# Half of the first K through ScalarE's DMA queue in float32 with a cast on chip, and batch 0's and 1's attention at other steps

## The chip, the cores and the metric

The kernel runs on one core of a Trainium2 chip. Times are device microseconds of that core. Each version is timed in rounds beside the kernel before on the same chip. A profile is of one execution; its span is about 1.8 us shorter than the time of the same run (511.5 against 513.26 us for the kernel before), so spans are compared with spans only.

## The reference

Inputs: q, k, v of 8 batches x 8 heads x 1024 tokens x 64; E and F of 64 x 1024; two FFN weights. All are float32.

```python
k_proj = einsum('ks,bhsd->bhkd', E, k)       # 1024 tokens -> 64
v_proj = einsum('ks,bhsd->bhkd', F, v)
attn   = softmax(q @ k_proj^T / 8)           # per head, over the 64
x      = attn @ v_proj                       # regrouped as (8192 tokens, 512)
out    = relu(x @ w_in) ** 2 @ w_out         # 512 -> 2048 -> 512
```

## The kernel before

All matrix work is bfloat16. GpSimd's queue loads q, k, v and the weights and casts them from float32 on the way; only E comes in float32 through SyncE's queue. The FFN of a batch runs in two halves of 512 tokens ("chunks" c), each with 16 first blocks (`fb`) of four matmuls and then the second matmuls. The order on TensorE is written by hand: the FFN is a generator that yields after each "step", and `at(step, ...)` puts pieces of the next batch's attention between steps. `warm(n)` issues n matmuls of zeros, only to keep TensorE busy.

```python
e_f32 = soft_pool.tile([KP, S], F32, tag="rs", name="e_f32")
nc.sync.dma_start(e_f32[:], E[:])
...
for g in range(2):
    load(K0[:, half[g]], tokens(k, 0, h=half[g]))            # load = nc.gpsimd.dma_start, casts
    load(Q0[:, half[g], 0:4, :], tokens(q, 0, h=half[g], i=slice(0, 4)))
    if g == 0:
        make_identity(nc, ident[:])
        load(f_bf[:], F[:])
for g in range(2):
    load(V0[:, half[g]], tokens(v, 0, h=half[g]))
# then w_in in five pieces, w_out in four, Q's second part before the last of them, batches 1, 2 ...
...
def sums(self, pr):                    # two head pairs at once
    ...                                # ones-matmuls of 32 rows into one tile
    nc.scalar.activation(rs[1][:], ps[:], AF.Ln)
    nc.scalar.activation(rs[0][:], rs[1][:], AF.Exp, scale=-1.0)
    nc.scalar.activation(rs[1][:], rs[1][:], AF.Exp, scale=-1.0)
    for j in range(2):
        for a in range(2):             # spread 32 rows to 64
            nc.vector.tensor_copy(rs[j][lack:lack + 32], rs[j][have:have + 32])
...
def chunk_sums(self, c, g):            # one at a time: Ln, Exp, no copies
    ps = att_psum()
    self.sums_mm(ps, self.e[g])
    self.rs[g] = self.inverse(ps)
```

The softmax here doesn't subtract the row's maximum and nothing guards it: scores larger than these inputs give would overflow.

Of the kernel before, what the change touches and what calls it, by code (L numbers as in the profile page):

```python
# [8 lines left out]
P = 128  # L9
F32 = mybir.dt.float32  # L10
# [8 lines left out]
def kernel(  # L19
# [49 lines left out]
    def bank(shape=(P, 512), dtype=F32):  # L69
        return fps.tile(list(shape), dtype, tag="bank", name="ps_bank")  # L70

    def tokens(src, b, h=slice(None), i=slice(None)):
        return src[b].rearrange("h (p i) d -> p h i d", i=NI)[:, h, i, :]

    def load(t, src):
        return nc.gpsimd.dma_start(t, src)  # L76
# [9 lines left out]
    e_f32 = soft_pool.tile([KP, S], F32, tag="rs", name="e_f32")  # L86
    nc.sync.dma_start(e_f32[:], E[:])

    K0, Q0, V0 = (qkv_pool.tile([P, H, NI, D], BF16, name=n) for n in ("K_sb", "Q_sb", "V_sb"))
    f_bf = soft_pool.tile([KP, S], BF16, tag="expT", name="f_bf")  # L90
    half = (slice(0, 4), slice(4, 8))
    ident = const_pool.tile([P, P], BF16, name="ident")
    for g in range(2):
        load(K0[:, half[g]], tokens(k, 0, h=half[g]))
        load(Q0[:, half[g], 0:4, :], tokens(q, 0, h=half[g], i=slice(0, 4)))
        if g == 0:
            make_identity(nc, ident[:])
            load(f_bf[:], F[:])
# [33 lines left out]
    def projection(name, e_bf):  # L132
        ps = bank([P, NI, KP], BF16)
        view = e_bf[:].rearrange("k (p i) -> k i p", i=NI)
        for i in range(NI):
            nc.tensor.transpose(ps[:, i, :], view[:, i, :], ident[0:KP, 0:KP])
        t = const_pool.tile([P, NI, KP], BF16, name=name)
        nc.vector.tensor_copy(t[:], ps[:])
        return t

    def warm(n):

        ps = bank()
        for _ in range(n):
            nc.tensor.matmul(ps[:], lhsT=zeros[:, 0:P], rhs=zeros[:], start=True, stop=True)
# [199 lines left out]
    class Ffn:  # L345
# [29 lines left out]
        def steps(self):  # L375
            for c in range(2):
                self.hsq[c] = hsq_pool.tile([P, NFB, TCH], BF16, name="hsq")
                first = self.cold and c == 0
                fb0 = 0
                if first:  # L380

                    banks = [bank() for _ in range(4)]
                    for g, fbs in ((0, (0, 1)), (0, (2, 3)), (1, (0, 1)), (1, (2, 3))):
                        for fb in fbs:
                            for cb in (2 * g, 2 * g + 1):
                                self.first_mm(c, fb, cb, banks[fb])
                            if g == 1:
                                self.square(c, fb, banks[fb])
                        yield
                    fb0 = 4  # L390
                for fb in range(fb0, NFB):
                    ps = bank()
                    for cb in range(NCB):
                        self.first_mm(c, fb, cb, ps)
                    self.square(c, fb, ps)
                    yield
                if first:

                    for t0 in range(0, 4, 2):
                        banks = [bank() for _ in range(2)]  # L400
                        for j in range(WP):
                            for t in range(2):
                                for fb in range(j * fn, (j + 1) * fn):
                                    self.second_mm(c, t0 + t, fb, banks[t])
                                if j == WP - 1:
                                    self.store(c, t0 + t, banks[t])
                                yield
                else:
                    last = self.b == B - 1 and c == 1
                    for tb in range(4):  # L410
                        if last and tb == 3:

                            for m in (slice(0, DM // 2), slice(DM // 2, DM)):
                                ps = bank()
                                for fb in range(NFB):
                                    self.second_mm(c, tb, fb, ps, m)
                                self.store(c, tb, ps, m)
                            break
                        ps = bank()
                        for j in range(WP):  # L420
                            for fb in range(j * fn, (j + 1) * fn):
                                self.second_mm(c, tb, fb, ps)
                            if j == WP - 1:
                                self.store(c, tb, ps)
                            yield

    with tc.manual_schedule(engines={PE}):
        e_bf = soft_pool.tile([KP, S], BF16, tag="expT", name="e_bf")
        nc.vector.tensor_copy(e_bf[:], e_f32[:])
        warm(8)  # L430
        ET = projection("ET", e_bf)
        warm(3)
        att = Attention(0)
        att.project_k(0)
        att.transpose_q_chunk(0, Q0, 0)
        att.transpose_k((0,))
        warm(1)
        att.chunk_scores(0, 0)
        FT = projection("FT", f_bf)
        att.project_k(1)  # L440
        att.chunk_sums(0, 0)
        att.transpose_q_chunk(0, Q0, 1)
        att.transpose_k((1,))
        warm(2)
        att.chunk_scores(0, 1)
        warm(4)
        att.project_v(0)
        att.chunk_sums(0, 1)
        warm(1)
        att.chunk_values(0, 0)  # L450
        warm(1)
        att.project_v(1)

        coming = None
        for b in range(B):
            plan = {}

            def at(step, fn, *args, **kwargs):
                plan.setdefault(step, []).append(lambda: fn(*args, **kwargs))

            if b == 0:
                at(1, att.chunk_values, 0, 1)
                at(20, att.transpose_q_chunk, 1, Q0, 0)
                at(20, att.transpose_q_chunk, 1, Q0, 1)
                at(22, att.chunk_scores, 1, 0)
                at(22, att.chunk_scores, 1, 1)
                at(25, att.chunk_sums, 1, 0)
                at(25, att.chunk_sums, 1, 1)
                at(29, att.chunk_values, 1, 0)
                at(29, att.chunk_values, 1, 1)  # L470
                nxt = Attention(1)
                nxt.load()
            if b + 1 < B:
                if b + 2 < B:
                    coming = Attention(b + 2)
                    coming.load()
                if b == 0:
                    at(36, nxt.project)
                    at(37, nxt.transpose_q, 0)
                    at(37, nxt.transpose_q, 1)  # L480
                    at(39, nxt.transpose_k)
                    at(41, nxt.scores, 0)
                    at(41, nxt.scores, 1)
                    at(43, nxt.transpose_q, 2)
                    at(43, nxt.transpose_q, 3)
                    at(45, nxt.sums, 0)
                    at(45, nxt.values, 0)
                    at(51, nxt.values, 1, True)
                    at(51, nxt.scores, 2)
                    at(51, nxt.scores, 3)  # L490
                    at(55, nxt.sums, 2)
                    at(55, nxt.values, 2)
                    at(55, nxt.values, 3, True)
                else:
                    at(14, nxt.scores, 0)
                    at(14, nxt.scores, 1)
                    at(18, nxt.sums, 0)
                    at(18, nxt.values, 0, True)
                    at(18, nxt.scores, 2)
                    at(27, nxt.values, 1)  # L500
                    at(27, nxt.scores, 3)
                    at(49, nxt.sums, 2)
                    at(49, nxt.values, 2)
                    at(49, nxt.values, 3, True)
                if b + 2 < B:
                    if b == 0:
                        at(61, coming.project)
                        at(63, coming.transpose_q_dma)
                        at(64, coming.transpose_k)
                    else:  # L510
                        at(27, coming.project)
                        at(30, coming.transpose_q_dma)
                        at(29, coming.transpose_k_dma)
            for step, _ in enumerate(Ffn(att, b == 0).steps(), 1):
                for stage in plan.pop(step, []):
                    stage()
            assert not plan, plan
            att, nxt = nxt, coming
# [30 lines left out]
```

## Time and profile before

| | kernel before |
|---|---|
| median of the first 3 runs | 513.74 us (513.23 to 514.64) |
| span of the profiled run | 511.5 us |
| first FFN matmul | 20.88 us |
| third w_in piece first used | 25.23 us |
| batch 1's first FFN matmul | 91.94 us |

From the page of the kernel before: TensorE's busy time, its granted clock and the DMA engines' share in 40 slices, and the chain of waits by engine.

```profile
PE 502.2 (98%) x2756; PEld 223.6 (44%) x2756; DVE 213.6 (42%) x433; ACT 273.7 (54%) x412; POOL 32.1 (6%) x44
...
PEclk9999999999999999999999999999999999999999
DMA  9999999899996199104931060100102011010102
...
PE 87%; DMA 11%; issue 1%; DVE 0%; POOL 0%; ACT 0%; POOLq 0%; ACTq 0%
```

TensorE is busy 98% of the span. The DMA line shows the engines full in most of the first 16 slices, which is 205 us, and rarely after. To see where TensorE lacks work, read its timeline. The columns are start, duration, engine, line, operation, output and inputs, count, and in brackets the idle time before it with what ended that. `ET` is E transposed, `xT` the attention's result, transposed, which the FFN reads; `ps_bank` and `ps_att` are TensorE's output buffers. TensorE at the start, kernel before:

```profile
5.23 0.68 PE L136 MATMUL ps_bank<-ident,e_bf 64*128 64x64 bf16 x8 [0.44 <-DVE e_bf L429]
...
7.29 1.03 PE L194 MATMUL ps_bank<-K_sb,ET 128*64 128x256 bf16 x8 [0.62 <-DMA K_sb<-in_k_dram]
...
11.85 1.88 PE L194 MATMUL ps_bank<-K_sb,ET 128*64 128x256 bf16 x8 [0.59 <-DMA K_sb<-in_k_dram]
...
20.88 1.04 PE L358 MATMUL ps_bank<-xT,w_in_114 128*128 128x512 bf16 x4
...
23.72 0.81 PE L358 MATMUL ps_bank<-xT,w_in_114 128*128 128x512 bf16 x3 [0.22 <-DVE xT L341]
...
25.23 3.62 PE L358 MATMUL ps_bank<-xT,w_in_118 128*128 128x512 bf16 x16
```

The eight K projections take 1.03 us at 7.29 us but 1.88 us at 11.85 us: the clock is halved there, which the records of the granted clock give as 0.5 from 11.92 to 15.33 us. The first FFN block over w_in_114 begins at 20.88 us, its second half waits for xT until 23.72 us, and the third piece, w_in_118, begins at 25.23 us.

TensorE's longest waits in the same trace (total, times, longest):

```profile
PE ps_bank L194 <- DMA K_sb<-in_k_dram: 1.2, 2, 0.6
...
PE ps_bank L241 <- DMA Q_sb<-in_q_dram: 0.8, 1, 0.8
PE ps_att L256 <- DVE xT L316: 0.8, 1, 0.8
PE ps_bank L231 <- DMA Q_sb<-in_q_dram: 0.7, 2, 0.4
```

Apart from the starting phase there are three: 0.82 us for batch 1's Q (L241), 0.44 us of the 0.7 for batch 0's second Q part (L231), and 0.76 us for an attention buffer that the xT multiply frees (L256). The chain of waits, in order of time (start, length, what):

```profile
3.86 7.94 DMA K_sb<-in_k_dram
...
12.09 16.78 DMA w_in_122<-in_moe_w_in_dram
...
29.15 30.96 DMA Q_sb<-in_q_dram
60.16 1.07 PE ps_bank L241 x16
```

Until 60.16 us the chain is one load after another on GpSimd's queue. From there on it is TensorE, but for the work of ScalarE and VectorE from 72.5 to 77.2 us that ends in the wait for the attention buffer.

### The profile page before, as it was taken

How to read it: one execution, taken by the hardware profiler on the slowest of the kernel's cores; microseconds unless marked ns; L12 is line 12 of the kernel's file. 1: busy time of each engine (PE TensorE's matmuls, PEld its weight loads, DVE VectorE, ACT ScalarE, POOL GpSimd, SP SyncE). 2: the span in 40 equal slices, each digit the busy share in tenths (PEclk: the TensorE clock that was granted, in tenths of full speed). 3: DMA queues.
4: the chain of work that ended last, by engine and by line, in shares of the span. 5: the costliest groups of instructions: out<-in, count | busy, mean ns of one | idle time of the engine just before them, and what ended most of it. 6: DMA issues, size and time to landing. Idle time of an engine off the chain costs nothing.

```text
span 511.5 us, 6926 instructions
## 1 busy us (share of the span) xinstructions
PE 502.2 (98%) x2756; PEld 223.6 (44%) x2756; DVE 213.6 (42%) x433; ACT 273.7 (54%) x412; POOL 32.1 (6%) x44
## 2 busy tenths in 40 slices
PE   7999999999999999999999999999999999999997
PEld 3444444444444444444444444444444444444444
DVE  2441666544444445345352354434443443522130
ACT  2565475673637556375654837366472755544351
POOL 7320100121000020001000000000000000000000
PEclk9999999999999999999999999999999999999999
DMA  9999999899996199104931060100102011010102
GB/s 161 204 205 222 227 207 201 129 217 205 195 214 124 43 183 210 71 0 91 201 88 45 1 161 16 60 24 32 63 1 81 2 41 42 25 59 21 62 1 82
DMA packets 67840, 53.92 MB, mean 105 GB/s; under 512 B 29152, under 2 KB 59616, under 8 KB 67808
## 3 DMA queue, kind: packets, MB, share of 16 engines
q0 software_dynamic: 30880, 29.49, 36.4%
q1 hardware_dynamic: 36928, 23.99, 17.8%
q8 instruction: 21, 0.34, 0.3%
q14 instruction: 11, 0.09, 0.1%
HBM read 59.24 MB, written 16.78 MB: 149 GB/s over the span
## 4 chain that ended last, share of the span: by engine, by line
PE 87%; DMA 11%; issue 1%; DVE 0%; POOL 0%; ACT 0%; POOLq 0%; ACTq 0%
PE ps_bank L364 40%; PE ps_bank L358 40%; DMA Q_sb<-in_q_dram 6%; DMA w_in_122<-in_moe_w_in_dram 3%; PE ps_bank L185 2%; DMA K_sb<-in_k_dram 2%; PE ps_att L256 1%; PE ps_att L290 1%; PE ps_att L312 1%; PE ps_bank L312 1%; PE ps_bank L241 0%; DVE rs L300 0%; ACT rs L296 0%; POOL K_sb L76 0%; DVE xT L316 0%
## 5 line engine op out<-in xcount | busy, mean ns | idle before, releaser
L355 DVE TENSOR_TENSOR hsq<-h_relu 128x512 bf16<-128x512 bf16 x256 | 108.7, 425 | 192.5 <-ACT h_relu L354 191.8
L354 ACT ACTIVATE h_relu<-ps_bank 128x512 bf16<-128x512 f32 x256 | 151.8, 599 | 69.5 <-PE ps_bank L358 69.4
L364 PEld LDWEIGHTS <-hsq 128*128 128x128 bf16 x1040 | 99.7, 98 | 122.9 <-issue 9.3
L371 ACT COPY o_sb<-ps_bank 128x512 f32<-128x512 f32 (+1 forms) x65 | 37.5, 579 | 111.1 <-PE ps_bank L364 105.0
L364 PE MATMUL ps_bank<-w_out_128,hsq 128*128 128x512 bf16 (+1 forms) x260 | 65.8, 376 | 0.0
L364 PE MATMUL ps_bank<-w_out_124,hsq 128*128 128x512 bf16 (+1 forms) x260 | 65.7, 376 | 0.0
L364 PE MATMUL ps_bank<-w_out_131,hsq 128*128 128x512 bf16 (+1 forms) x260 | 65.6, 376 | 0.0
L364 PE MATMUL ps_bank<-w_out_126,hsq 128*128 128x512 bf16 (+1 forms) x260 | 65.6, 376 | 0.0
L358 PE MATMUL ps_bank<-xT,w_in_122 128*128 128x512 bf16 x256 | 59.1, 379 | 0.0
L358 PE MATMUL ps_bank<-xT,w_in_118 128*128 128x512 bf16 x256 | 58.2, 379 | 0.0
L358 PE MATMUL ps_bank<-xT,w_in_120 128*128 128x512 bf16 x256 | 58.2, 379 | 0.0
L300 DVE COPY rs<-rs 32x1024 f32<-32x1024 f32 x56 | 38.6, 690 | 42.3 <-ACT rs L295 41.5
L270 ACT ACTIVATE expT<-ps_att 128x1024 bf16<-128x1024 f32 x32 | 31.8, 1023 | 25.3 <-PE ps_att L256 25.2
L358 PEld LDWEIGHTS <-w_in_122 128*128 128x128 bf16 x256 | 24.5, 98 | 31.2 <-issue 2.7
L358 PEld LDWEIGHTS <-w_in_120 128*128 128x128 bf16 x256 | 24.9, 98 | 30.1 <-issue 0.4
L358 PEld LDWEIGHTS <-w_in_118 128*128 128x128 bf16 x256 | 24.9, 98 | 29.9 <-issue 0.4
L358 PE MATMUL ps_bank<-xT,w_in_114 128*128 128x512 bf16 x128 | 30.6, 379 | 0.2 <-DVE xT L341 0.2
L358 PE MATMUL ps_bank<-xT,w_in_116 128*128 128x512 bf16 x128 | 30.4, 379 | 0.0
L316 DVE TENSOR_TENSOR xT<-ps_att,rs 128x512 bf16<-128x512 f32 x28 | 18.1, 686 | 9.2 <-PE ps_att L312 8.9
L294 ACT ACTIVATE rs<-ps_att 128x1024 f32<-128x1024 f32 x14 | 14.3, 1023 | 12.7 <-PE ps_att L290 12.7
L358 PEld LDWEIGHTS <-w_in_114 128*128 128x128 bf16 x128 | 12.4, 98 | 15.3 <-issue 0.9
L358 PEld LDWEIGHTS <-w_in_116 128*128 128x128 bf16 x128 | 12.4, 98 | 15.1 <-issue 0.2
(71 smaller groups left out, 236.6 us busy)
## 6 DMA issues: line engine op xcount, KB each, us to landing
out_dram<-o_sb SPq DMA_DIRECT2D x63, 256.0 KB, 2.0
K_sb<-in_k_dram POOLq DMA_DIRECT2D x7, 1024.0 KB, 22.2
V_sb<-in_v_dram POOLq DMA_DIRECT2D x7, 1024.0 KB, 26.7
Q_sb<-in_q_dram POOLq DMA_DIRECT2D x7, 1024.0 KB, 14.8
K_sb<-in_k_dram POOLq DMA_DIRECT2D x2, 512.0 KB, 7.0
V_sb<-in_v_dram POOLq DMA_DIRECT2D x2, 512.0 KB, 11.1
Q_sb<-in_q_dram POOLq DMA_DIRECT2D x2, 256.0 KB, 7.5
w_in_118<-in_moe_w_in_dram POOLq DMA_DIRECT2D x1, 512.0 KB, 14.9
```

The lines of the kernel that those rows point to most:

```text
L185: nc.tensor.matmul(ps[LO, :], lhsT=ET[:, i, :], rhs=self.K[:, :, i, :], start=f, stop=l)
L256: nc.tensor.matmul(ps[o, par], lhsT=self.kT[r, h % 4, h // 4, :], rhs=self.qT[r, h, n, :], start=True, stop=True)
L270: nc.scalar.activation(e[:], ps[:], AF.Exp, scale=SCALE)
L294: nc.scalar.activation(rs[1][:], ps[:], AF.Ln)
L300: nc.vector.tensor_copy(rs[j][lack:lack + 32], rs[j][have:have + 32])
L312: nc.tensor.matmul(ps_x[par][o], lhsT=self.vp[r, 2 * pr + a, :], rhs=e[r, par], start=True, stop=True)
L316: nc.vector.tensor_tensor(out=self.xT[:, pr, :, par], in0=ps_x[par].rearrange("p (c t) -> p c t", c=2), in1=rs[:, par].rearrange("p (c t) ...
L354: nc.scalar.activation(r[:], ps[:], AF.Relu)
L355: nc.vector.tensor_tensor(out=self.hsq[c][:, fb, :], in0=r[:], in1=r[:], op=ALU.mult)
L358: nc.tensor.matmul(ps[:], lhsT=w_in_blk(cb, fb), rhs=self.xT[:, cb, c].rearrange("p a t -> p (a t)"), start=(cb == 0), stop=(cb == NCB - 1),)
L364: nc.tensor.matmul(ps[:, m], lhsT=self.hsq[c][:, fb, tb * P:(tb + 1) * P], rhs=w_out_blk(fb)[:, m], start=(fb == 0), stop=(fb == NFB - 1),)
L371: nc.scalar.copy(o[:, m], ps[:, m])
```

## The change

The intent is to bring batch 0's first K half in over a second queue, so that the other loads begin one transfer earlier, and to place the attention of batches 0 and 1 so that TensorE never waits for a load.

```diff
+    k_f32 = []
+    for j in range(2):
+        t = soft_pool.tile([P, 2, NI, D], F32, tag="rs", name="k_f32")
+        nc.scalar.dma_start(t[:], tokens(k, 0, h=slice(2 * j, 2 * j + 2)))
+        k_f32.append(t)
...
     for g in range(2):
-        load(K0[:, half[g]], tokens(k, 0, h=half[g]))
+        if g == 1:
+            load(K0[:, half[g]], tokens(k, 0, h=half[g]))
...
-                    banks = [bank() for _ in range(4)]
-                    for g, fbs in ((0, (0, 1)), (0, (2, 3)), (1, (0, 1)), (1, (2, 3))):
-                        for fb in fbs:
+                    banks = [bank() for _ in range(2)]
+                    for g in range(2):
+                        for fb in range(2):
...
-                    fb0 = 4
+                    fb0 = 2
...
         nc.vector.tensor_copy(e_bf[:], e_f32[:])
+        nc.vector.tensor_copy(K0[:, 0:2], k_f32[0][:])
+        nc.scalar.copy(K0[:, 2:4], k_f32[1][:])
...      # warm(n) in the start: 3 -> 4 after ET, 0 -> 1, 1 -> 3, 0 -> 3 after FT, 4 -> 2, 0 -> 1, 1 -> 0
             if b == 0:
-                at(20, att.transpose_q_chunk, 1, Q0, 0)      # and ..., 1)
-                at(22, att.chunk_scores, 1, 0)               # and 1, 1
-                at(25, att.chunk_sums, 1, 0)                 # and 1, 1
+                at(21, att.transpose_q_chunk, 1, Q0, 0)
+                at(23, att.chunk_scores, 1, 0)
+                at(26, att.sums, 0)
...
-                    at(37, nxt.transpose_q, 0)               # and 1
+                    at(39, nxt.transpose_q, 0)
-                    at(43, nxt.transpose_q, 2)               # and 3
+                    at(44, nxt.transpose_q, 2)
-                    at(45, nxt.values, 0)
-                    at(51, nxt.values, 1, True)
-                    at(51, nxt.scores, 2)
+                    at(48, nxt.values, 0, True)
+                    at(48, nxt.scores, 2)
+                    at(51, nxt.values, 1)
```

More of the change, by code (lines that the diff above doesn't have):

```diff
@@ L429 @@
         nc.vector.tensor_copy(e_bf[:], e_f32[:])
+        nc.vector.tensor_copy(K0[:, 0:2], k_f32[0][:])
+        nc.scalar.copy(K0[:, 2:4], k_f32[1][:])
         warm(8)
         ET = projection("ET", e_bf)
-        warm(3)
+        warm(4)
         att = Attention(0)
         att.project_k(0)
+        warm(1)
         att.transpose_q_chunk(0, Q0, 0)
         att.transpose_k((0,))
-        warm(1)
+        warm(3)
         att.chunk_scores(0, 0)
         FT = projection("FT", f_bf)
+        warm(3)
         att.project_k(1)
@@ L445 @@
         att.chunk_scores(0, 1)
-        warm(4)
+        warm(2)
         att.project_v(0)
+        warm(1)
         att.chunk_sums(0, 1)
-        warm(1)
         att.chunk_values(0, 0)
@@ L462 @@
                 at(1, att.chunk_values, 0, 1)
-                at(20, att.transpose_q_chunk, 1, Q0, 0)
-                at(20, att.transpose_q_chunk, 1, Q0, 1)
-                at(22, att.chunk_scores, 1, 0)
-                at(22, att.chunk_scores, 1, 1)
-                at(25, att.chunk_sums, 1, 0)
-                at(25, att.chunk_sums, 1, 1)
+                at(21, att.transpose_q_chunk, 1, Q0, 0)
+                at(21, att.transpose_q_chunk, 1, Q0, 1)
+                at(23, att.chunk_scores, 1, 0)
+                at(23, att.chunk_scores, 1, 1)
+                at(26, att.sums, 0)
                 at(29, att.chunk_values, 1, 0)
@@ L478 @@
                     at(36, nxt.project)
-                    at(37, nxt.transpose_q, 0)
-                    at(37, nxt.transpose_q, 1)
+                    at(39, nxt.transpose_q, 0)
+                    at(39, nxt.transpose_q, 1)
                     at(39, nxt.transpose_k)
@@ L483 @@
                     at(41, nxt.scores, 1)
-                    at(43, nxt.transpose_q, 2)
-                    at(43, nxt.transpose_q, 3)
+                    at(44, nxt.transpose_q, 2)
+                    at(44, nxt.transpose_q, 3)
                     at(45, nxt.sums, 0)
-                    at(45, nxt.values, 0)
-                    at(51, nxt.values, 1, True)
-                    at(51, nxt.scores, 2)
+                    at(48, nxt.values, 0, True)
+                    at(48, nxt.scores, 2)
+                    at(51, nxt.values, 1)
                     at(51, nxt.scores, 3)
```

## The prediction

> **What bounds the kernel now.** TensorE: busy 98% of a 511.5 us span (the page's first part), and the chain of waits is TensorE matmuls back to back from 60.2 us to the end. In the timeline, 16 steady 512-column matmuls take 3.45 us at a granted clock of 1.00, gapless after 77.6 us. The diff leaves batches 2 to 7 alone, so only the first 78 us can change. There the chain is one DMA queue: loads land back to back until 60.2 us at about 205 GB/s of bfloat16 (windows view), twice that as float32 read.
>
> **What can be won,** by TensorE's timeline:
> - Start-up: the first FFN matmul starts at 20.88 us. K's second half is waited for until 11.85 us; from 12 to 15.5 us the granted clock is about 0.5: eight 256-column matmuls take 1.88 us, against 1.03 us for the first half. Being cold costs about 1.3 us there (0.85 + 0.4 on transposes + 0.2 on sums).
> - Three stalls: 0.44 us for Q's second part (39.6), 0.82 us for batch 1's Q (60.2), 0.76 us for a buffer that the xT multiply frees (77.2).
>
> **What the change does.**
> 1. 1 MB of float32 K leaves GpSimd's queue (one 0.89 us issue less before everything else there). The bytes read are the same. ScalarE issues it after its 1.28 us table load, so no earlier than before. The Trainium skill ("DMA: Bandwidth & Descriptors", Queues, rings and completion order) says that each engine takes its queues in turn, so K now shares with Q, F and the second K half. No run shows it yet. Casts add about 0.7 us on VectorE (64x1024 took 0.69) and an estimated 1.0 us on ScalarE (128x1024 activations take 1.02). Net: first K ready at 7.5 to 9 us (7.29 now), Q and F earlier, the second K half at 11 to 12 us.
> 2. Five more warm-up matmuls keep the clock full. "TensorE: Matmul & The Clock Gate" (Part 1) has the array drop to half clock after an idle window of about 3.4 us; the trace agrees (0.50 after a sparse stretch). Gain about 1.3 us.
> 3. Only two FFN blocks, not four, are now begun before the first group's xT is whole. That gives back about 0.8 us. Net start-up gain 0.6 us.
> 4. Q's transposes move one step (0.86 us) and batch 1's two to three steps (1.7 us) later: 0.44 + 0.82 us of stalls go.
> 5. The joint sums of batch 0 save 0.2 us of matmul, but add four 0.69 us VectorE copies before xT. Sums end near 46.2; Ln and two exponentials to 49.4, copies to 51.2, four multiplies to 53.8, while the second FFN half wants xT from 51.9: a new stall of about 1.2 us.
> 6. The new place of batch 1's values removes the 0.76 us stall.
>
> Sum: 0.6 + 1.26 + 0.2 - 1.2 + 0.76 = about 1.6 us, all on the critical path, of 513.74.
>
> **Predicted: 512.1 us, 8 in 10 between 510.4 and 514.1.** Faster by over 2%: 0.005; within 2%: 0.985; slower: 0.01.
>
> **What would show it.** Granted clock near 1.0 from 12 to 15.5 us; first FFN matmul near 19.5 us; no TensorE wait for Q; at about 52 us a TensorE wait on the xT multiply of around 1 us; no stall near 77; equal matmul spacing after 80 us.
>
> **What would make it wrong.** K on ScalarE's queue landing after 9 us (the two queues halving each other); V or w_in landing so late that a faster start only waits; the step-5 stall being absent (then about 511) or costing the clock (then above 513).

## The result, and the profile after

| | before | after |
|---|---|---|
| median | 513.52 us (6 runs, 513.23 to 514.64) | 513.00 us (6 runs, 512.56 to 513.18) |
| span of the profiled run | 511.5 us | 511.2 us |

The ratio is 0.9986, with a 95% interval of 0.9973 to 0.9999: the same within 2%, a little faster. Ratios are the mean time of one kernel's runs over the mean of the other's in the same rounds, so they are not quite the ratio of the medians.

The same lines of the page, kernel after:

```profile
PE 502.9 (98%) x2761; PEld 223.9 (44%) x2761; DVE 217.5 (43%) x438; ACT 273.7 (54%) x412; POOL 31.2 (6%) x43
...
PEclk8999999999999999999999999999999999999999
DMA  9999999899996199104941060100102011010102
...
PE 96%; DVE 1%; DMA 1%; ACT 0%; issue 0%; ACTq 0%; DVEq 0%
```

The chain of waits is now 96% TensorE, and the DMA part fell from 11% to 1%. So the change did take the loads off the chain. It still saved only half a microsecond. To see why, here is the start on TensorE, kernel after (L201 is the K projection, L365 the first FFN matmul):

```profile
6.72 0.68 PE L143 MATMUL ps_bank<-ident,e_bf 64*128 64x64 bf16 x8 [1.93 <-DVE e_bf L436]
...
8.30 1.89 PE L201 MATMUL ps_bank<-K_sb,ET 128*64 128x256 bf16 x8
...
21.36 1.04 PE L365 MATMUL ps_bank<-xT,w_in_117 128*128 128x512 bf16 x4
...
23.61 0.38 PE L365 MATMUL ps_bank<-xT,w_in_117 128*128 128x512 bf16 x1 [0.87 <-DVE xT L348]
...
26.58 3.62 PE L365 MATMUL ps_bank<-xT,w_in_121 128*128 128x512 bf16 x16
```

TensorE's longest waits after the change:

```profile
PE ps_bank L143 <- DVE e_bf L436: 1.9, 1, 1.9
PE ps_bank L365 <- DVE xT L348: 1.8, 5, 0.9
```

The waits for Q and the one for the attention buffer are gone. New ones stand in their place, for E's cast and for xT. Of the 1.8 us for xT, 0.87 and 0.22 us lie at 23.6 and 24.2 us, where two blocks are too few to fill the time until xT's second half (the kernel before, with four, waits 0.22 us there); the other three, of 0.22 us each, lie at the FFN's second half. The start across engines, kernel after (SPq and ACTq are the queues' issue instructions):

```profile
0.74 1.28 ACT L108 ACT_TABLE_LOAD   x1 [0.74 <-PEq L543]
0.74 0.57 SPq L87 DMA_DIRECT2D e_f_91<-in_E_dram  x1
0.77 0.45 ACTq L92 DMA_DIRECT2D k_f_93<-in_k_dram  x1
...
1.25 0.49 ACTq L92 DMA_DIRECT2D k_f_95<-in_k_dram  x1
...
5.96 0.71 DVE L436 CAST e_bf<-e_f_91 64x1024 bf16<-64x1024 f32 x1 [4.74 <-DMA e_f_91<-in_E_dram]
...
6.92 1.05 ACT L438 CAST K_sb<-k_f_95 128x1024 bf16<-128x1024 f32 x1 [4.89 <-DMA k_f_95<-in_k_dram]
```

E and the first K piece are issued within 0.03 us of each other, and K's issue runs while ScalarE loads its table. E's cast begins at 5.96 us (4.48 us before). The chain of waits from 0 to 90 us begins with it:

```profile
0.74 5.19 DMA e_f_91<-in_E_dram
5.96 0.72 DVE e_bf L436
```

The new wait at the FFN's second half comes from the joint sums (the softmax denominators of two head pairs at once). VectorE and then TensorE, kernel after:

```profile
49.85 2.79 DVE L307 COPY rs<-rs 32x1024 f32<-32x1024 f32 x4 [6.66 <-ACT rs L302]
52.68 2.49 DVE L348 TENSOR_TENSOR xT<-ps_att,rs 128x512 bf16<-128x512 f32 x4
```

```profile
53.43 0.38 PE L365 MATMUL ps_bank<-xT,w_in_117 128*128 128x512 bf16 x1
54.02 0.38 PE L365 MATMUL ps_bank<-xT,w_in_117 128*128 128x512 bf16 x1 [0.22 <-DVE xT L348]
54.62 0.38 PE L365 MATMUL ps_bank<-xT,w_in_117 128*128 128x512 bf16 x1 [0.22 <-DVE xT L348]
55.22 1.24 PE L365 MATMUL ps_bank<-xT,w_in_117 128*128 128x512 bf16 x5 [0.22 <-DVE xT L348]
```

VectorE spends 2.79 us on four copies of the joint sums. Then each of the first four FFN matmuls waits for its own xT multiply.

A ledger of where TensorE begins the same work in both traces (us):

| TensorE begins | before | after | after minus before | what lies between |
|---|---|---|---|---|
| first FFN matmul | 20.88 | 21.36 | +0.48 | E late, half clock earlier |
| third w_in piece | 25.23 | 26.58 | +1.35 | two blocks instead of four |
| second w_out matmuls, second pair of token blocks | 44.67 | 45.41 | +0.74 | no wait for Q |
| second half's first FFN matmul | 52.90 | 53.43 | +0.53 | joint sums |
| second half's second w_in piece | 54.63 | 56.30 | +1.67 | the wait for xT |
| second half's fourth w_in piece | 63.87 | 64.55 | +0.68 | no wait for batch 1's Q |
| after batch 1's last values | 81.99 | 81.81 | -0.18 | no wait for the buffer |
| batch 1's first FFN matmul | 91.94 | 91.77 | -0.17 | nothing |

The plan of steps won about what it should, and the start and the joint sums gave nearly all of it back. The 0.17 us that are left at batch 1 stay to the end: TensorE's last matmul ends at 507.96 us, against 508.13 before. The rest of the 0.3 us between the two spans comes after it, and the 0.5 us between the medians is larger still; no trace here explains that part.

### The profile page after: what moved, and what is told of

The parts are those of the page before. It is cut to its first block, busy times and chain, and to the rows that moved or that the text cites. A ratio compares the mean times of both kernels' runs of the same rounds, so it can differ in the third digit from the quotient of the medians.

```text
span 511.2 us, 6948 instructions
## 1 busy us (share of the span) xinstructions
PE 502.9 (98%) x2761; PEld 223.9 (44%) x2761; DVE 217.5 (43%) x438; ACT 273.7 (54%) x412; POOL 31.2 (6%) x43
## 4 chain that ended last, share of the span: by engine, by line
PE 96%; DVE 1%; DMA 1%; ACT 0%; issue 0%; ACTq 0%; DVEq 0%
PE ps_bank L365 43%; PE ps_bank L371 43%; PE ps_bank L192 2%; PE ps_att L263 2%; DMA e_f_91<-in_E_dram 1%; PE ps_att L297 1%; PE ps_att L319 1%; PE ps_bank L152 1%; PE ps_bank L319 1%; DVE xT L348 1%; PE ps_bank L201 1%; PE ps_bank L238 0%; PE ps_bank L211 0%; PE ps_bank L248 0%; DVE rs L307 0%
## 5 line engine op out<-in xcount | busy, mean ns | idle before, releaser
L307 DVE COPY rs<-rs 32x1024 f32<-32x1024 f32 x60 | 41.7, 695 | 47.1 <-ACT rs L302 46.2
L365 PE MATMUL ps_bank<-xT,w_in_125 128*128 128x512 bf16 x256 | 59.1, 379 | 0.0
L365 PE MATMUL ps_bank<-xT,w_in_123 128*128 128x512 bf16 x256 | 58.0, 379 | 0.0
L365 PE MATMUL ps_bank<-xT,w_in_121 128*128 128x512 bf16 x256 | 58.0, 379 | 0.0
L365 PEld LDWEIGHTS <-w_in_123 128*128 128x128 bf16 x256 | 25.0, 98 | 30.4 <-issue 0.4
L365 PEld LDWEIGHTS <-w_in_121 128*128 128x128 bf16 x256 | 24.9, 98 | 30.2 <-issue 0.4
L365 PEld LDWEIGHTS <-w_in_125 128*128 128x128 bf16 x256 | 24.4, 98 | 31.0 <-issue 2.7
L365 PE MATMUL ps_bank<-xT,w_in_117 128*128 128x512 bf16 x128 | 31.0, 379 | 1.8 <-DVE xT L348 1.8
L365 PE MATMUL ps_bank<-xT,w_in_119 128*128 128x512 bf16 x128 | 30.2, 379 | 0.0
L365 PEld LDWEIGHTS <-w_in_117 128*128 128x128 bf16 x128 | 12.4, 98 | 17.2 <-issue 3.2
L365 PEld LDWEIGHTS <-w_in_119 128*128 128x128 bf16 x128 | 12.5, 98 | 15.1
```

The lines of the kernel that those rows point to most:

```text
L365: nc.tensor.matmul(ps[:], lhsT=w_in_blk(cb, fb), rhs=self.xT[:, cb, c].rearrange("p a t -> p (a t)"), start=(cb == 0), stop=(cb == NCB - 1),)
```

## The experiments

Eleven versions ran, in three groups, each on one chip with the kernel before (r1 on one chip, r2 and r3 on another; the record doesn't name the chip of the changed kernel's own runs). The groups differ little: the median of the kernel before was 513.52, 513.64 and 513.67 us. "Position" is the start of batch 1's first FFN matmul in the profiled run (91.94 before, 91.77 after).

| run | median us (range) | ratio to before (95%) | first FFN | position |
|---|---|---|---|---|
| after | 513.00 (512.56-513.18) | 0.9986 (0.9973-0.9999) | 21.36 | 91.77 |
| r1_start_only | 512.99 (512.85-513.11) | 0.9987 (0.9974-1.0001) | 22.26 | 91.87 |
| r1_plan_only | 512.98 (512.26-513.92) | 0.9988 (0.9974-1.0001) | 20.88 | 91.10 |
| r1_split_sums | 512.22 (511.90-513.02) | 0.9975 (0.9962-0.9987) | 21.61 | 91.08 |
| r1_k_behind_e | 515.68 (514.87-516.11) | 1.0036 (1.0023-1.0048) | 24.14 | 94.54 |
| r2_warm_13 | 511.71 (511.57-512.51) | 0.9964 (0.9952-0.9976) | 20.00 | 90.45 |
| r2_split_four | 512.07 (511.13-512.97) | 0.9964 (0.9949-0.9978) | 21.11 | 89.72 |
| r2_old_start_split | 512.24 (511.36-512.45) | 0.9967 (0.9955-0.9979) | 20.89 | 90.00 |
| r2_early_scores | 512.37 (511.73-513.10) | 0.9974 (0.9961-0.9986) | 20.71 | 90.41 |
| r3_three | 511.21 (510.65-511.93) | 0.9949 (0.9937-0.9961) | 20.24 | 89.89 |
| r3_three_out8 | 510.75 (510.54-511.06) | 0.9941 (0.9928-0.9954) | 20.00 | 89.39 |
| r3_old_loads_out8 | 511.57 (511.03-512.80) | 0.9957 (0.9944-0.9970) | 20.49 | 89.97 |

### The two parts alone

Plan only: the kernel before with the changed `if b == 0` plan and nothing else.

> The plan of steps of the changed kernel on the start-up of before (SWDGE load of K, four FFN blocks, old warm-ups). Theory A (the plan gains about 1.5 us, the new start-up gives about 1.35 us of it back): 512.0 us, 1.5 us under before and 1.0 us under the changed kernel; third w_in piece first used at 25.2 us as before; no wait for Q; an xT wait of about 1.1 us at the second FFN half. Rival B (the start-up gains 0.6 us as I predicted and the plan nothing): 513.5 us.

Start only: the changed loads, casts and warm-ups, with four blocks and the plan of before.

> The new loads, casts and warm-ups with four FFN blocks and the plan of before. Theory A: first FFN matmul again near 21.4 us (20.88 before), third w_in piece first used near 25.7 us, and a total of 513.5 us, within 0.4 us of before, because the stalls for Q and for batch 1's Q swallow half a microsecond of lateness. Rival B: 512.9 us.

Measured: 512.98 and 512.99 us. Neither theory got both totals right. The plan alone moved the position by 0.84 us (91.94 to 91.10), not by 1.5. Its trace shows where the rest went, a new wait for the last w_out piece:

```profile
42.34 1.02 PE L364 MATMUL ps_bank<-w_out,hsq 128*128 128x512 bf16 x4 [0.52 <-DMA w_out<-in_moe_w_out_dram]
```

With the first wait for Q removed, TensorE reaches the next load at 41.8 us. That this was too early is also chance: the piece landed at 42.30 us in this profile, and at 41.69 us in that of the kernel before. The profiled run was the slowest of its five, and a second cost stands far behind the position, near 154 and 156 us, where TensorE waits for ScalarE to free a result bank (the cause comes below, under "Four blocks again"):

```profile
PE ps_bank L358 <- ACT o_sb L371: 1.2, 2, 1.0
```

The start alone is more instructive. Its first FFN matmul came 1.4 us later than before (22.26 against 20.88 us), and at batch 1 the position was 91.87 us against 91.94: the delay had vanished, because in the old plan TensorE then has nothing to wait for at either Q. That this start was 0.9 us later than the same start in the changed kernel (21.36 us) belongs to this execution and not to the start: here the four warm-ups after E's transposes already ran at half clock (1.89 instead of 1.04 us), there the half clock began only after them. Four profiles of this start have the first FFN matmul at 21.11 to 22.26 us. In the plan of before, lateness at the start is free up to more than a microsecond, since loads set the pace until 60 us. In the changed plan it isn't: TensorE needs batch 1's Q at 62.57 us, it landed at 59.78 us, and nothing waits.

### The joint sums

```diff
-                at(26, att.sums, 0)
+                at(26, att.chunk_sums, 1, 0)
+                at(26, att.chunk_sums, 1, 1)
```

> The changed kernel with batch 0's second-chunk sums as two separate calls again, at the changed step 26. Theory: the four VectorE copies (2.79 us) go, the 1.15 us xT wait at 53.4 us goes to under 0.3 us, 0.2 us of matmul come back: 512.1 us, 0.9 us under the changed kernel. Rival (the wait is only taken over by the later load of batch 1's Q or by another buffer): within 0.3 us of the changed kernel.

Measured: 512.22 us, 0.8 us under the changed kernel, and the position 0.69 us earlier although this run's start was 0.25 us later. The sixteen FFN matmuls of the second half now run in one piece:

```profile
53.88 3.62 PE L365 MATMUL ps_bank<-xT,w_in 128*128 128x512 bf16 x16
```

The theory holds. The joint sums save 0.2 us of matmuls and one activation of ScalarE (1.06 us), but here the path to xT counts, and 2.79 us of VectorE copies lie on it. The run takes out the joint sums as a whole; that the copies are what costs is read from the trace.

### Why E is late

```diff
-        nc.scalar.dma_start(t[:], tokens(k, 0, h=slice(2 * j, 2 * j + 2)))
+        nc.sync.dma_start(t[:], tokens(k, 0, h=slice(2 * j, 2 * j + 2)))
```

> The changed kernel with the two float32 K pieces issued behind E on SyncE's queue. Theory (E is late, 5.96 against 4.48 us, because K's data overtook or shared with it; TensorE then stands idle 1.9 us and drops to half clock until 12 us): E lands near 4.5 us, K's second piece near 7 us, first K projection still near 8.2 us but at full clock (8 matmuls in about 1.05 us instead of 1.89), first FFN matmul near 20.3 us, total 512.1 us. Rival (E's lateness has another cause, or the clock is paid back by a later wait): within 0.3 us of the changed kernel.

Measured: 515.68 us, slower by 2.7 us. One half of the theory held: E's cast began at 4.48 us again, as in the kernel before, so it was K's data that made E late. The other half fell: K's second piece was cast only at 10.03 us, and TensorE stood idle for 4.26 us.

```profile
5.22 0.67 PE L143 MATMUL ps_bank<-ident,e_bf 64*128 64x64 bf16 x8 [0.64 <-DVE e_bf L436]
...
11.12 1.86 PE L201 MATMUL ps_bank<-K_sb,ET 128*64 128x256 bf16 x8 [4.26 <-ACT K_sb L438]
```

The trace's packet records, summed by queue, show how the queues shared the engines. Kilobytes that landed in each half microsecond (GpSimd's are bfloat16 as written, half of what it reads):

```
from us    after: E / K (ScalarE) / GpSimd     K behind E: E+K (SyncE) / GpSimd
 2.5            0 / 180 /   0                      114 /   0
 3.0            0 / 204 /   0                      184 /   0
 3.5          102 /  65 /   0                      122 /   0
 4.0          139 /  20 /   0                      186 /   0
 4.5           20 /  90 /   0                      176 /  14
 5.0            0 / 153 /   0                        2 /  95
 5.5            0 / 198 /   1                        4 /  95
 6.0            0 /  61 /  61                       98 /  45
 6.5            0 /   0 /  96                      116 /  35
 7.0            0 /   0 /  89                       71 /  65
```

In the changed kernel the order is K's first piece, E (beside the end of that piece), K's second piece, and only then GpSimd's queue, whose first load was issued by 2.13 us and moved its first data at 5.91 us. E's first packet started at 3.53 us, K's at 1.87 us. So K's pieces arrived early because they went ahead of everything, and E paid. Once K was behind E, its second piece ran beside GpSimd's loads and finished at 9.69 us instead of 6.48 us.

### The idle TensorE at the start

```diff
-        warm(8)
+        warm(13)
```

> The changed kernel with 13 instead of 8 warm-up matmuls before E's transposes, so that TensorE has work while E is late; nothing else moves. Theory (in the changed kernel TensorE is behind the loads from the start to the end, so a start saved is a microsecond saved): no half clock between 8 and 12 us, first FFN matmul near 20.5 us instead of 21.4, and the total falls by the same amount, to 512.2 us. Rival (the start is absorbed by the next wait for a load, as it was in the kernel before): the start moves, the total stays within 0.3 us of 513.0.

Measured: 511.71 us, ratio 0.9964. Five matmuls of zeros bring more than the whole change did. E is cast no earlier, and the K projection starts at the same 8.3 us:

```profile
6.72 0.68 PE L143 MATMUL ps_bank<-ident,e_bf 64*128 64x64 bf16 x8 [0.52 <-DVE e_bf L436]
...
8.29 1.06 PE L201 MATMUL ps_bank<-K_sb,ET 128*64 128x256 bf16 x8
...
20.00 1.04 PE L365 MATMUL ps_bank<-xT,w_in 128*128 128x512 bf16 x4
```

But it runs at full clock (1.06 us instead of 1.89), the first FFN matmul comes 1.36 us earlier than in the changed kernel, and the position is 1.32 us earlier. In the changed kernel the records give clock 0.5 from 8.37 to 11.78 us; in this run they give 1.0 from 5.34 us to almost the end. The rival, that the next wait for a load absorbs it, falls for this plan: all five runs (at most 512.51 us) lie below all six of the changed kernel (at least 512.56 us).

### Four blocks again

Split sums, with the four FFN blocks of the kernel before.

> The split-sums kernel with the four FFN blocks of before at the start. Theory (two blocks cost 0.87 us, since nothing fills the wait for the second half of the first xT, and that is on the critical path): third w_in piece first used 4.35 us after the first FFN matmul instead of 5.2, total 511.4 us. Rival (the second w_in piece is then waited for, which is why the change went to two blocks): 512.2 us, with a wait for w_in before 25 us.

Measured: the third w_in piece starts 4.35 us after the first FFN matmul (5.22 in the changed kernel), with no wait for w_in; that is the 0.87 us expected. The position fell by 1.36 us against the split sums, 0.50 of it by an earlier start in this run. Yet the median fell by only 0.15 us (0.27 us when each is taken against the kernel before on its own chip). The trace shows where it went, much later, on TensorE:

```profile
154.18 9.66 PE L365 MATMUL ps_bank<-xT,w_in 128*128 128x512 bf16 x44 [1.27 <-ACT o_sb L378]
```

and on ScalarE just before:

```profile
150.33 0.58 ACT L378 COPY o_sb<-ps_bank 128x512 f32<-128x512 f32 x1 [6.29 <-PE ps_bank L371]
153.54 0.58 ACT L378 COPY o_sb<-ps_bank 128x512 f32<-128x512 f32 x1 [2.63 <-DMA out_dram<-o_sb]
```

ScalarE's copy of an output waits 2.63 us for a free output buffer, and so the FFN's next block waits 1.27 us. The packet records say why the store was late. Stores (packets of 2048 bytes) and the DMA transposes of the next Q (packets of 256 bytes) share SyncE's queue. From 121 to 148 us that queue moved only 256-byte packets, about 40 kB per us beside 150 to 160 kB per us of GpSimd's loads, though stores had been issued at 137.5, 142 and 143 us. The longest store there took 12.8 us to land; the median store of the whole kernel before takes 2.0. Here, too, loads set the pace: from 106 to 110 us, with hardly any load beside them, such 256-byte packets moved at 174 to 285 kB per us. In the kernel before ScalarE waits 5.6 us at 151.9 us for the same reason, but TensorE doesn't. An earlier start alone doesn't decide whether TensorE waits: r2_warm_13, at position 90.45, has no such wait, and r1_plan_only, at 91.10, has 1.2 us of it. What does decide is not shown.

### The old loads with the new plan

The kernel before with the changed plan, the sums split; and the same with scores and sums one step earlier.

```diff
-                at(23, att.chunk_scores, 1, 0)      # and 1, 1
-                at(26, att.chunk_sums, 1, 0)        # and 1, 1
+                at(22, att.chunk_scores, 1, 0)
+                at(25, att.chunk_sums, 1, 0)
```

> K loaded as before (one queue, cast in the load), the warm-ups and four blocks of before; only the changed plan of steps, with the second-chunk sums split. Theory (loading K through ScalarE's queue brings the loads of batch 0 no earlier, and makes E late): the stream of loads lands as in the kernel before, a wait of about 0.5 us for the last w_out piece near 42 us, no xT wait at 53 us; total 511.3 us, equal or better than the split-sums kernel with four blocks. Rival (the new loads are what makes the plan possible): slower than that kernel by 0.5 us or more.

> The same with batch 0's second-chunk scores and sums one step earlier, so that the scores stand before the first use of the last w_out piece. Theory: the wait of 0.5 us for that piece shrinks by up to 0.4 us; total 511.0 us. Rival: the scores now wait for VectorE's copies of Q and give the same back; within 0.2 us of the kernel without it.

Measured: 512.24 and 512.37 us. The first waited 0.33 us for the last w_out piece and, like the version before it, 1.0 us at 154 us for the output buffer, so its total says little about the loads. It lies within 0.2 us of the split sums with four blocks, so the two ways of loading K aren't told apart here. The earlier scores removed the wait for w_out, but TensorE then waited 0.55 us for batch 1's Q, and 0.6 us for the output buffer. That is within noise of the first, as the rival said. Whether the edit brought the wait for Q is not shown: in this profile the loads were late from the start (the first K projection at 8.09 instead of 7.35 us), and batch 1's Q landed at 61.15 us instead of 60.67.

### All three repairs, the output buffers, and the loads once more

r3_three: the changed kernel with `warm(13)`, split sums and four blocks. r3_three_out8 also has:

```diff
-    out_pool = ctx.enter_context(tc.tile_pool(name="outp", bufs=4))
+    out_pool = ctx.enter_context(tc.tile_pool(name="outp", bufs=8))
```

r3_old_loads_out8 takes r3_three_out8, loads K's first half by GpSimd's queue again, and has 8 warm-ups before and 6 after E's transposes.

> The changed kernel with all three repairs: 13 warm-up matmuls, split second-chunk sums, four FFN blocks. Alone they moved TensorE's position at batch 1's first FFN matmul by 1.3, 0.7 and 0.9 us. Theory (there is a second place where loads set the pace, near 153 us: ScalarE's output copies wait for buffers, whose stores stand on SyncE's queue behind a DMA transpose that waits for a late load of Q): the position near 91 us falls to about 89.3 us, the last w_out piece is waited for about 0.5 us at 41.7 us, and a stall of 1.3 to 1.7 us appears near 154 us; total about 511.5 us. Rival (the gains add up): 510.2 us.

> The same with eight output buffers instead of four. Theory: ScalarE's copies no longer wait for stores, the stall near 154 us goes, total 510.0 us and less spread between runs. Rival (the stall comes from something else there, or the next wait is right behind it): within 0.3 us of the run with four buffers.

> As that, but with K loaded as before (GpSimd's queue, cast in the load), eight warm-ups before E's transposes and six after. Theory (the new place of K's load brings no load earlier and only delays E): position near 91 us and total within 0.3 us of the run with the new loads, 510.0 us. Rival (the new loads do help once their E problem is repaired): slower by 0.5 us or more.

Measured: 511.21, 510.75 and 511.57 us. With four buffers TensorE waited 0.73 us at 153.8 us, less than expected, perhaps because this run's start was late (it waited 0.46 us for V). With eight the wait was gone, and the runs were closer together (0.5 instead of 1.3 us); the median was 0.46 us lower, which is within the spread of the first. TensorE's waits in that run, all of them:

```profile
PE ps_bank L152 <- DVE zeros L110: 1.2, 1, 1.2
PE ps_bank L371 <- DMA w_out<-in_moe_w_out_dram: 0.6, 1, 0.6
PE ps_bank L365 <- DVE xT L348: 0.2, 1, 0.2
PE ps_att L263 <- DVE kT L226: 0.2, 1, 0.2
```

Only 0.6 us for the last w_out piece is left that a load causes. This is the fastest version, 2.9 us (0.59%) under the kernel before and 2.25 us under the changed kernel as it was (in another group).

The last run was to decide about K's loads, and its time speaks against my theory. With the old loads the median is 0.8 us higher. TensorE waits for V's second half:

```profile
PE ps_bank L204 <- DMA V_sb<-in_v_dram: 1.4, 1, 1.4
...
PE ps_bank L364 <- DMA w_out<-in_moe_w_out_dram: 0.6, 1, 0.6
```

The packet records agree in sign, though not in size. Counting what had been read through all load queues, everything up to V was in at 17.0 to 17.4 us in the seven profiles with K on ScalarE's queue, and at 17.5 to 17.7 us in four of the five with the old loads (18.3 us in r2_early_scores). K's early data uses the time from 2 to 6 us, in which the kernel before moves 0.67 MB by 5 us and the changed one 0.90. Later the lead is no longer clear: the last w_out piece landed at 41.5 to 42.0 us in the seven, and at 41.7 to 42.5 us in the five. Nor does the wait for V belong to the old loads alone. V's second half landed at 19.45 us in this run and at 18.25 us in the kernel before; with the new loads it was 17.8 to 18.0 us in four profiles, but 18.7 to 19.2 us in the three with 13 warm-ups. Why it came late there I couldn't tell. r3_three, with the new loads, had the position 89.89, this run 89.97. So the gain of 0.8 us in time is measured, and its cause stays open; some 0.5 us of it can be read from the packets (everything up to V in at 17.03 against 17.56 us in these two profiles).

## Why the prediction was right or wrong

The time was inside the range (513.0 in 510.4 to 514.1), and the class was right; no change at all (513.5) would have been inside it too. The point, 512.1, was 0.9 us too low, and the traces show a larger miss: of the 1.6 us foretold, 0.17 us arrived at batch 1. That the median came 0.5 us down is in part luck, since no step of the prediction accounts for the rest. The start missed by 1.95 us (steps 1 to 3), and the other steps came out 0.5 us better than foretold. The miss at the start goes back to one step.

1. *What bounds the kernel*: right. Loads set the pace to 60 us, and the start's lateness vanished in r1_start_only as it must then.
2. *K through ScalarE's queue* (step 1): the failed step. "ScalarE issues it after its 1.28 us table load, so no earlier than before" was wrong: the issue stood at 0.77 us, during the table load, and K's first data moved at 1.87 us (3.20 us before, on GpSimd's queue). I had looked for harm in K landing late beside Q, F and the second K half. In fact K's pieces went ahead of all of them, K's second piece was cast by 7.97 us, within the range I gave, and the one transfer behind it was E, which I hadn't listed. E landed 1.5 us later.
3. *Warm-ups* (step 2): wrong, as a consequence. "Five more warm-up matmuls keep the clock full" failed because the idle 1.93 us came before them: all five stand behind E's transposes. The half clock moved from 11.92-15.33 us to 8.37-11.78 us; it did not go. r2_warm_13, at full clock, began the FFN 1.36 us earlier than the changed kernel, which is the 1.3 us predicted.
4. *Two blocks* (step 3): right, 0.87 us against "about 0.8". Summed up, the start was to gain 0.6 us and lost 1.35 us at the third w_in piece: an error of two microseconds.
5. *The waits for Q* (step 4): right; the ledger shows 0.61 and 0.99 us, where I had 0.44 and 0.82.
6. *The joint sums* (step 5): right. The wait was 1.14 us against "about 1.2", and at the place named.
7. *Batch 1's values* (step 6): right, 0.86 us against 0.76.

Summed from the ledger: 1.35 - 0.61 - 0.21 + 1.14 - 0.99 - 0.86 = -0.18 us. The profiled spans differ by 0.3 us and the medians by 0.5 us.

On "TensorE: Matmul & The Clock Gate", Part 1: the page gives free-running windows of 3413 ns and a drop after an idle one. The traces agree on the length: the half-clock stretch is 3.41 us before and after, and twice that (6.83 us) in r1_k_behind_e. But the window before the drop need not be wholly idle: in the changed kernel the 3.41 us before it (4.95 to 8.37 us) hold 1.77 us without work, and then E's transposes and four warm-ups. In r2_warm_13, with 0.52 us without work, the clock stayed full.

## What to carry to other kernels

When loads set the pace, a faster or slower start is hidden; when a new order takes those waits away, the start counts in full, so repair it in the same change (here five matmuls of zeros were worth 1.3 us). A transfer put on a second queue can go ahead of small transfers that everything else needs: list every transfer issued in the same microsecond, and look at which one the first matmul needs. After each gain, look for the next place where loads or stores set the pace, here, in r2_split_four, a wait for output buffers 60 us later that took 1.27 of the 1.36 us gained.

## What the Trainium skill lacked or had wrong

- "DMA: Bandwidth & Descriptors", Queues, rings and completion order: it says that each engine goes round-robin among the queues it has work for. In the changed kernel GpSimd's queue had its first data packet at 5.91 us, though its load was issued by 2.13 us, while K and E from the other two queues went nearly as whole transfers, one after the other. In r1_k_behind_e the queues did share from 6 us on (98 against 45 kB in the first half microsecond). No run here shows what decides between the two.
- The same page, Issuing engines are not separate DMA queues: it says that issuing from several engines saves only the sequencer's time. It gives no figure for what that is worth at the start of a kernel. Here one K piece of 0.5 MB took 0.45 us to issue on ScalarE, and the half of 1 MB 0.89 us on GpSimd in the kernel before; the reading was ahead by 0.1 to 0.7 us up to V, leaving out r2_early_scores. No run separates the issue's time from the queue's own.
- "ScalarE: Activation LUTs", What ACT_TABLE_LOAD costs: it gives about 1283 ns, as measured here (1.28 us). It doesn't say that ScalarE's DMA issues go out during the load (0.77 and 1.25 us, inside 0.74 to 2.02 us).
- No page that I read gives a figure for stores that stand behind DMA transposes on the same issuing queue, beside loads: 27 us (121 to 148 us in r2_split_four) of 256-byte packets at about 40 kB per us, and a store that took 12.8 us to land.
